# A planned attention and MLP kernel: three score groups of the last batch in one 64-row stretch, a plan that counts descriptors, and another order of the first loads

## The chip, the cores and the metric

The kernel runs on one core of one Trainium2 chip. The metric is the device time of one execution in microseconds (us), median of the runs of a kernel. A profile is one further execution recorded by the hardware profiler; its times are counted from the first instruction of its span. Engines: PE is TensorE (PEld its weight loads, SPq and ACTq are the DMA issues of the SyncE and ScalarE queues), ACT is ScalarE, DVE VectorE, POOL GpSimd, SP SyncE.

## What is computed

Sliding-window attention over 8 batches of 8 heads, 576 positions and head size 64, then a two-layer network with squared ReLU over all 4608 tokens:

```python
scores = q @ k.transpose / sqrt(64)              # batch, head, 576 x 576
mask = abs(pos[:, None] - pos[None, :]) <= 32    # else -1e9
attn = softmax(where(mask, scores, -1e9))
x = (attn @ v).transpose(0, 2, 1, 3).reshape(4608, 512)
g = maximum(x @ w_in, 0) ** 2                    # w_in 512 x 2048
out = g @ w_out                                  # w_out 2048 x 512, float32 out
```

Inputs are float32 in DRAM; the matmuls run in bf16 with float32 sums.

## The kernel before

**Tiles.** A batch has three attention groups of 192 queries; group G runs from 0 to 23. A group works on two windows (A and B) of 128 keys. `scores` (line 548) makes both windows' scores for 8 heads: 16 matmuls with 64 rows of contraction (the head size) and 128 columns. Heads with even and odd number lie in rows 0 to 63 and 64 to 127 and write two different PSUM banks; the code calls the two row halves in turn. Both windows fill the whole 128x2048 PSUM tile `at`. ScalarE takes the exponential of 1024 columns for each window (line 573) into one of two tiles `e`, VectorE multiplies with the band mask (line 578) into one of three tiles `pt`, and `pv` (line 606) multiplies with V: 8 matmuls of 65 columns, the 65th of which is the sum of the softmax. They write into the same tile `at`. VectorE divides (lines 625 and 628) into `xa` (64 tokens) and `xb` (128 tokens), and clears half of the tile (line 634).

**From attention to network.** `xturn` transposes `xa` and `xb` into `xt`, features by tokens: for groups 0 to 2 on TensorE, from group 3 on by two DMA transposes on SP's queue (lines 701 and 704). `mm1` (line 721) is the first product for a chunk of tokens: 192 tokens up to token 767, 256 up to 2047, then 512; for 128 features of the hidden layer it takes four matmuls, and 64 for the chunk. ScalarE's ReLU (727) and VectorE's square (730) write `gt`, with hidden features in partitions. `mm2` (741) is the second product for a block u of 128 tokens, in four quarters of four matmuls, each with 128 rows and 512 columns, into PSUM tile `outp` u modulo 2; ScalarE evicts (751) and stores. The last block is cut in three (`mm2_last`, 766).

**Loads.** POOL issues the loads that cast to bf16. The first six groups' Q and K come in pairs of rows (`load_pair`, 410) and are transposed on TensorE (469); batch 0 group 0 comes over SP without a cast. From batch 2 on they come as 128-row pieces (378) and are transposed by DMA on SP (509). The first loads, with W1 and W2 in quarters (440, 445) and V (427), stand in `OPENING`.

**The plan.** Every operation is recorded (`rec`) with engine, cost, key (its due time) and data dependences. `schedule` then plays the program through with a model of engines and DMA rings and at each step gives a free engine the ready operation with the smallest key. The order that comes out, engine by engine, is the program; `emit` puts in semaphore waits. The times of the model are in no instruction: the constants at the top shape the order alone. Attention has keys of 3G - LEAD, the first product token/64, the second 2u + LAG. Where TensorE would stand still early on, `idle` matmuls are put in (313).

In the text, T4b is group 4's second transpose on SP, and so on.

Of the kernel before, what the change touches and what calls it, by code (L numbers as in the profile page):

```python
# [22 lines left out]
LEAD = 13.0  # L23
LAG = 9.0
AHEAD = 9.0
TISS = 1340
TMOVE = 15
NVR = 24
VKEY = 10.0
TSLACK = 3500  # L30
# [4 lines left out]
PQ = 100  # L35
# [4 lines left out]
HOLD = {}  # L40
# [5 lines left out]
HWB = 150  # L46
# [3 lines left out]
FIRST = {}  # L50
T512 = 2048
NBIAS = 1
PKEY = 0.2
MKEY = (-9.5, -6.5)
VSET = (-9.8, -6.8)
ESPLIT = 0
IOTA = -1
OPENING = [("k", 1), ("w1", 0), ("v", 0, 0), ("v", 1, 1), ("q", 1), ("v", 0, 1), ("q", 2), ("k", 2), ("v", 1, 0), ("w1", 1),
           ("w1", 2), ("w1", 3), ("q", 5), ("v", 2, 0), ("v", 2, 1), ("w2", 1), ("k", 3), ("v", 3, 0), ("q", 3), ("w2", 0), ("w2",
           2), ("k", 4), ("v", 3, 1), ("q", 4), ("v", 5, 0), ("v", 5, 1), ("w2", 3), ("hq", 0), ("k", 5), ("v", 4, 0), ("v", 4, 1),  # L60
           ("hk", 0)]
# [3 lines left out]
KC = ((0, 224), (224, 192), (416, 160))  # L65


class Op:
    __slots__ = ("eng", "fn", "deps", "order", "inc", "val", "sem", "dma", "dur", "key", "i",
                 "succ", "left", "ready", "start", "end", "lat", "move", "name", "slack")  # L70


class Prog:
# [5 lines left out]
    def __init__(self, nc):  # L79
        self.nc = nc  # L80
        self.ops = []
        self.writer = {}
        self.readers = {}

    def rec(self, eng, fn, reads=(), writes=(), dma=None, dur=100, key=0.0, move=0, name="", after=None, slack=0, war=()):
# [5 lines left out]
        op.slack = slack  # L91
        op.lat = self.LAT[eng]
# [24 lines left out]

    def schedule(self):
        ops = self.ops
        for op in ops:  # L120
            op.succ, op.left, op.ready = [], 0, 0
# [15 lines left out]
        now = spent = 0.0  # L137

        def done(op, end):
            for s in op.succ:  # L140
                s.ready = max(s.ready, end if op in s.deps or op.eng != s.eng else free[op.eng])
                s.left -= 1
                if not s.left:
                    heapq.heappush(wait[s.eng], (s.ready, s.i, s))

        def serve(until):
            nonlocal now, spent
            while now < until:
# [16 lines left out]
                if it[1] <= 0:  # L165
                    rings[q].pop(0)
                    it[3].end = now + LANDQ + it[3].slack
                    done(it[3], it[3].end)
                    return True
            return False  # L170

        while True:
            best = None
            for e in engs:
                if pool[e]:
# [13 lines left out]
            if serve(t):  # L189
                continue  # L190
            while wait[e] and wait[e][0][0] <= t:
                _, i, op = heapq.heappop(wait[e])
                heapq.heappush(pool[e], (op.key, i, op))
            first = pool[e][0]
            soon = min((w[0] for w in wait[e] if t < HOLDT and w[0] <= t + HOLD.get(e, 0) and w[2].key < first[0] - KMIN), default=None)
            if soon is not None and soon - t < first[2].dur:
                free[e] = soon
                continue
            op = heapq.heappop(pool[e])[2]
# [8 lines left out]
        assert len(out) == len(ops)  # L208
        self.length = max(o.end for o in out)
        at = free["PE"] = 1500  # L210
        for op in sorted((o for o in out if o.eng == "PE"), key=lambda o: o.start):
            gap = min(op.start, WARM, self.idle_end.start) - at
            one = 430 if at < 5000 else 230
            for k in range(int((gap - 60) // one)):
                w = Op()
                w.eng, w.fn, w.dma, w.deps, w.i = "PE", self.idle, None, {self.idle_on}, op.i
                w.inc, w.val, w.sem, w.start, w.end, w.dur, w.key = False, None, None, at + one * k, 0, one, -99
# [5 lines left out]
    def emit(self):  # L223
        nc = self.nc
        engs = {"PE": nc.tensor, "ACT": nc.scalar, "DVE": nc.vector, "POOL": nc.gpsimd, "SP": nc.sync}
        for op in self.ops:
            for d in op.deps:
                if d.dma is None and not (d.eng == "PE" and op.eng == "PE"):
                    d.inc = True
        sems = {e: nc.alloc_semaphore(f"s_{e}") for e in engs}  # L230
# [6 lines left out]
        for op in self.ops:  # L237
            e = engs[op.eng]
            need = {}
            for d in op.deps:  # L240
                if d.dma is None and d.eng == "PE" and op.eng == "PE":
                    continue
                need[d.sem] = max(need.get(d.sem, 0), d.val)
# [27 lines left out]
class Gen:  # L271
# [5 lines left out]
    def alloc(self):  # L277
# [14 lines left out]
        self.PT = [sb(f"pt{i}", [128, 8, 128], BF16) for i in range(3)]  # L292
# [224 lines left out]
    def scores(self, G, ws):  # L517
# [3 lines left out]
        key = 3 * G - LEAD + 0.3 * ws[0]  # L521
# [39 lines left out]
        if G < NBIAS:  # L561
            rd += [t for w in ws for t in tags[w]]
        self.moe = self.p.rec("PE", f, reads=rd, writes=[t for w in ws for t in tags[w]], key=key, dur=190 + 235 * len(ws),
                              name=f"S{G}{'AB'[ws[-1]]}")
        for w in ws:
            n = 2 * G + w
            sc = self.AT[:, 1024 * reg[w]:1024 * reg[w] + 1024]
            e_, pt = self.E[n % 2], self.PT[n % 3]
            if G < NBIAS:
                self.p.rec("ACT", lambda e, pt=pt, sc=sc: e.activation(pt[:].rearrange("p h q -> p (h q)"), sc, ACTF.Exp, scale=0.125),  # L570
                           reads=tags[w], writes=[("pt", n % 3)], key=key, dur=act(1024), name=f"X{G}{'AB'[w]}")
# [7 lines left out]
                       reads=[("e", n % 2), ("mask", mi)], writes=[("pt", n % 3)], key=key, dur=dve(1024),  # L579
                       name=f"M{G}{'AB'[w]}")  # L580

    def pv(self, G, w):
        b, g = divmod(G, 3)
        n = 2 * G + w
        key = 3 * G - LEAD + 0.3 * w + 0.1
        reg = 1 if NBIAS <= G < NSPLIT or G < NDUP and w else 0
        c0 = 1024 * reg
        vt, pt, avp = self.V[G % NV], self.PT[n % 3], self.AT
# [3 lines left out]
        def f(e):  # L592
            if w and G < NDUP:
                for h in range(8):
                    x, y = divmod(h, 4)
                    c = c0 + 512 * x + 65 * y
                    e.matmul(avp[:, c:c + 65], self.PT[(n - 1) % 3][:, 4 * (h % 2) + h // 2, :], vt[:, 0, h, 0:65], start=(y == 0),
# [12 lines left out]
        rd = [("v", G % NV, w), ("vset", G % NV), ("pt", n % 3), "zz"]  # L610
# [4 lines left out]
        if G < NDUP and w:  # L615
            rd += [("pt", (n - 1) % 3), ("v", G % NV, 0)]
# [19 lines left out]
    def xturn(self, G):  # L636
        xa, xb = self.XA[G % 3], self.XB[G % 3]
        key = 3 * G - LEAD + 0.5
# [95 lines left out]
    def mm2(self, u, seg, key):  # L734
# [4 lines left out]
        def f(e):  # L739
            for d in range(4 * seg, 4 * seg + 4):  # L740
# [5 lines left out]
                       writes=[f"outp{u % 2}"], key=key, dur=864, name=f"B{u}.{seg}")  # L746
        if u == 1 and seg == 0 and not XTD:
# [35 lines left out]
    def build(self):  # L783
# [35 lines left out]
        todo = []  # L819

# [3 lines left out]
        for G in range(NG):  # L824
            b, g = divmod(G, 3)
            if b > 1:
                key = 3 * G - LEAD - AHEAD
# [4 lines left out]
                if g and G < NVR:  # L832
                    key = 3 * G - LEAD - 0.5 if G >= VCS else key
                    at(key + 0.01, self.copy_v, G, key - VKEY if G >= VCS else key)
            for t in "kq":
                key = 3 * G - LEAD - (0.6 if b < NTURN else 3)
                for c in (g,) if b < NTURN else PIECES[t][g]:
                    at(key, self.turn_pe if b < NTURN else self.turn_dma, t, b, c, key)
            for ws in ((0,), (1,)) if G < NSPLIT else ((0, 1),):
                at(3 * G - LEAD + 0.3 * ws[0], self.scores, G, ws)  # L840
            for w in range(2):
                at(3 * G - LEAD + 0.3 * w + 0.1, self.pv, G, w)
            at(3 * G - LEAD + 0.5, self.xturn, G)
# [15 lines left out]
        if True:  # L859
            dsems, dcount = p.emit()  # L860
            for s in dsems:
                if s[0] == "o":
                    self.nc.sync.wait_ge(dsems[s], dcount[s])
# [35 lines left out]
```

## Time and profile before

| | |
|---|---|
| runs without a profile | median 301.89 us (301.73 to 302.03, 3 runs) |
| the profiled execution, its own time | 302.86 us |
| its span, first to last instruction | 301.50 us |
| granted TensorE clock, mean | 1.000 |
| TensorE busy | 292.0 us |
| first product (L721), second product (L741) busy | 142.3 us, 134.2 us |
| scores (L548), V products (L606) busy | 15.2 us, 20.1 us |
| DMA packets, bytes | 160060, 39.83 MB |

Busy times of matmuls include a modelled end of each; what a matmul really holds up is seen from the distance to the start of the next. A timeline's row is: start, duration, engine, line, operation, tile written, shape, count; in brackets the idle time before it and what ended it. The row of a wait is: who waited for whom, us in total, times, longest. "DMA to landing" is the time from the start of an issue to the arrival of its data, least, median, most of a line's instructions in the window asked for.

### The profile page before, as it was taken

What the parts mean: (1) busy time and instruction counts of PE and PEld (TensorE: products, weight loads), DVE (VectorE), ACT (ScalarE), POOL (GpSimd) and SP (SyncE); (2) the same over time, 40 slices, a digit from 0 to 9 for tenths busy, and PEclk for the clock granted to TensorE, in tenths of its full rate; (3) what the DMA queues carried; (4) which work ended last, traced back from release to release, by engine and by line L of the source; (5) the groups of instructions that cost most, each with busy time, mean ns of one, the idle gap of its engine ahead of it and who ended that gap; (6) DMA issues with size and microseconds to landing.
All of it is one profiled execution on the core that took longest, in us unless ns stands there. A gap on an engine that the chain in (4) does not pass through costs nothing.

```text
span 301.5 us, 6221 instructions
## 1 busy us (share of the span) xinstructions
PE 292.0 (97%) x2394; PEld 171.4 (57%) x2431; DVE 166.6 (55%) x385; ACT 160.7 (53%) x250; POOL 102.6 (34%) x131
## 2 busy tenths in 40 slices
PE   7899999998999999999999999999999999999997
PEld 2578865846677777755444444444444444444445
DVE  6897785726666767664377756675465322222200
ACT  3587834825567646654566665456546344344312
POOL 8993335406542643654065435340000000000000
PEclk9999999999999999999999999999999999999999
DMA  9999999999998999999999999996211201000112
GB/s 168 176 206 184 195 173 174 171 154 187 189 157 144 163 145 171 142 163 187 206 144 134 158 164 123 197 164 134 63 34 44 81 35 37 35 35 36 37 70 104
DMA packets 160060, 39.83 MB, mean 132 GB/s; under 512 B 149408, under 2 KB 155552, under 8 KB 160032
## 3 DMA queue, kind: packets, MB, share of 16 engines
q0 software_dynamic: 105824, 17.93, 85.3%
q1 hardware_dynamic: 48880, 12.14, 28.8%
q10 hardware_dynamic: 5328, 9.37, 8.9%
q8 instruction: 19, 0.31, 0.5%
q14 instruction: 9, 0.07, 0.1%
HBM read 36.70 MB, written 9.44 MB: 153 GB/s over the span
## 4 chain that ended last, share of the span: by engine, by line
PE 90%; DMA 5%; POOL 3%; issue 1%; ACT 1%; POOLq 0%; ACTq 0%
PE ht L721 41%; PE outp L741 40%; DMA w<-in_moe_w_in_dram 5%; PE at L606 4%; PE at L548 3%; POOL v L427 1%; POOL w L440 1%; PE at L469 1%; PE ht L766 1%; PE outp L766 1%; POOL kpair L410 1%; POOL qpair L410 1%; ACT rt L727 0%; ACT oe L751 0%; ACT oe L776 0%
## 5 line engine op out<-in xcount | busy, mean ns | idle before, releaser
L721 PE MATMUL ht<-xt,w 128*128 128x256 bf16 (+2 forms) x886 | 142.3, 302 | 2.9 <-issue 1.3
L741 PE MATMUL outp<-w,gt 128*128 128x512 bf16 x535 | 134.2, 379 | 1.4 <-issue 0.2
L727 ACT ACTIVATE rt<-ht 128x512 bf16<-128x512 f32 (+1 forms) x152 | 86.4, 578 | 91.0 <-PE ht L721 87.0
L721 PEld LDWEIGHTS ht<-xt,w 128*128 128x128 bf16 x896 | 80.9, 98 | 44.8 <-issue 1.6
L730 DVE TENSOR_TENSOR gt<-rt 128x512 bf16<-128x512 bf16 (+1 forms) x152 | 61.4, 408 | 64.5 <-ACT rt L727 63.0
L741 PEld LDWEIGHTS outp<-w,gt 128*128 128x128 bf16 x560 | 52.3, 98 | 55.8 <-ACT oe L751 1.0
L378 POOL DMA_DIRECT2D kraw<-in_k_dram x30 | 25.3, 849 | 95.8 <-PE at L548 66.9
L573 ACT ACTIVATE e<-at 128x1024 bf16<-128x1024 f32 x46 | 44.9, 1023 | 10.9 <-PE at L548 10.8
L578 DVE TENSOR_TENSOR pt<-e,mask 128x1024 bf16<-128x1024 bf16 x46 | 31.5, 691 | 24.5 <-ACT e L573 24.2
L427 POOL DMA_DIRECT2D v<-in_v_dram x48 | 38.6, 824 | 0.0
L751 ACT ACTIVATE oe<-outp 128x512 f32<-128x512 f32 x35 | 21.1, 602 | 24.9 <-PE outp L741 24.9
L378 POOL DMA_DIRECT2D qraw<-in_q_dram x30 | 25.5, 859 | 0.0
L606 PEld LDWEIGHTS at<-v,pt 128*128 128x128 bf16 x384 | 18.0, 98 | 10.0 <-issue 1.4
L606 PE MATMUL at<-v,pt 128*128 128x65 bf16 x384 | 20.1, 194 | 0.5 <-ACT pt L570 0.5
L628 DVE TENSOR_TENSOR xb<-at,rs 128x512 bf16<-128x512 f32 x24 | 16.6, 691 | 1.0
L628 DVE TENSOR_TENSOR xa<-at,rs 64x512 bf16<-64x512 f32 x24 | 16.7, 695 | 0.8
L625 DVE RECIPROCAL rs<-at 64x8 f32<-64x8 f32 (+1 forms) x48 | 10.1, 209 | 10.2 <-PE at L606 8.6
L548 PEld LDWEIGHTS at<-qt,kt 64*128 64x128 bf16 x384 | 10.8, 94 | 8.3 <-issue 6.5
L548 PE MATMUL at<-qt,kt 64*128 64x128 bf16 x384 | 15.2, 217 | 0.1
L634 DVE MEMSET at<- 64x520 f32 x23 | 11.3, 492 | 3.7 <-DVE xa L628 2.9
L434 DVE COPY v<-v 64x512 bf16<-64x512 bf16 x16 | 6.1, 382 | 7.4 <-PE ht L721 6.1
L773 DVE COPY oe<-ht 128x128 f32<-128x128 f32 x1 | 0.3, 292 | 14.6 <-PE ht L766 14.6
(67 smaller groups left out, 82.9 us busy)
## 6 DMA issues: line engine op xcount, KB each, us to landing
out_dram<-oe ACTq DMA_DIRECT2D x35, 256.0 KB, 3.7
kraw<-in_k_dram POOLq DMA_DIRECT2D x24, 128.0 KB, 5.3
qraw<-in_q_dram POOLq DMA_DIRECT2D x24, 128.0 KB, 5.8
w<-in_moe_w_in_dram POOLq DMA_DIRECT2D x4, 512.0 KB, 11.5
v<-in_v_dram POOLq DMA_DIRECT2D x16, 128.0 KB, 7.1
w<-in_moe_w_out_dram POOLq DMA_DIRECT2D x4, 512.0 KB, 18.7
v<-in_v_dram POOLq DMA_DIRECT2D x16, 96.0 KB, 7.0
v<-in_v_dram POOLq DMA_DIRECT2D x16, 64.0 KB, 6.0
```

Source lines behind the costliest of these rows:

```text
L378: self.p.rec("POOL", lambda e: e.dma_start(raw[0:n, x % 2, :].rearrange("p (h d) -> p h d", h=8), s), writes=[("raw", t, x // 2, x % 2)], ...
L427: self.p.rec("POOL", lambda e, j=j, lo=lo, hi=hi, k0=k0: e.dma_start(vt[lo - k0:hi - k0, j, :, 0:64], self.v[b, :, lo:hi, :].rearrange("h ...
L548: mm = e.matmul(sc[:, 512 * par + 128 * j:512 * par + 128 * j + 128], kt[r:r + 64, j, k0:k0 + 128], q, start=G >= NBIAS, stop=True, skip_g ...
L573: self.p.rec("ACT", lambda e, e_=e_, sc=sc: e.activation(e_[:], sc, ACTF.Exp, scale=0.125), reads=tags[w], writes=[("e", n % 2)], key=key, ...
L578: self.p.rec("DVE", lambda e, pt=pt, ee=ee, mb=mb: e.tensor_tensor(pt[:], ee, mb, ALU.mult), reads=[("e", n % 2), ("mask", mi)], writes=[( ...
L606: mm = e.matmul(avp[:, c:c + 65], pt[:, 4 * (h % 2) + h // 2, :], vt[:, w, h, 0:65], start=(w == 0 and y == 0), stop=True, skip_group_chec ...
L628: self.p.rec("DVE", lambda e: e.tensor_tensor(x[r0:128, :].rearrange("p (x y c) -> p x y c", x=2, y=4), av[:, :, :, 0:64], rb, ALU.mult), ...
L721: mm = e.matmul(ht[:, n * x:n * x + n], self.W1[:, ft, 128 * d:128 * d + 128], self.XT[:, ft, r:r + n], start=(ft == 0), stop=(ft == 3))
L727: self.p.rec("ACT", lambda e: e.activation(rt[:, 0:c], ht[:, 0:c], ACTF.Relu), reads=[f"ht{k % 2}"], writes=[("rt", k % 4)], key=key, dur= ...
L730: self.p.rec("DVE", lambda e: e.tensor_tensor(gt[:, d0:d0 + len(ds), r:r + n], rr, rr, ALU.mult), reads=[("rt", k % 4)], writes=[("gt", s, ...
L741: mm = e.matmul(op[:], gt[:, d, r:r + 128], self.W2[:, d, :], start=(d == 0), stop=(d == 15))
L751: self.p.rec("ACT", lambda e: e.activation(oe, op[:], ACTF.Copy), reads=[f"outp{u % 2}"], writes=[("oe", u % 4)], key=key, dur=act(512), n ...
```

## The change

1. **A chain.** `CHAINS = {21: 3}`: the scores of groups 21, 22 and 23 are one sequence on TensorE. If the operands of the next two second-product blocks are ready in the plan, `fill` takes these blocks' eight quarters out and puts two runs `half_block(u, 0)` and `half_block(u, 1)` between the score groups: 32 matmuls each of 64 rows and 512 columns, row halves in turn, the two blocks in turn. In the first run block u takes rows 0 to 63 and block u+1 rows 64 to 127 of the hidden features, in the second the other way round; the second waits for the first by a semaphore (`fence`). A chain starts when its data is known, and other groups may be held back for it. `pt` has 7 tiles instead of 3, and the V products of the chained groups use both halves of `at` in turn.
2. **Chunks.** Tokens 768 to 1279 come in chunks of 192, 192 and 128.
3. **The plan.** It counts the descriptors of POOL's loads in flight and holds POOL's next load over 1024; other costs for DMA turns and transposes (`PQ`, `HWB`, `TMOVE`), `LEAD` 12.5 and `LAG` 9.5, ScalarE may be held up to 150 ns for a more urgent operation, batches 2, 6 and 7 get other due times.
4. **The opening.** W1's first quarter is issued first, ahead of the iota, then V, K, Q in another order.

What the built program shows: TensorE's instruction count is nearly the same, and in the stretch of group 21 to 23 it has 16 score matmuls, 32 of `half_block`, 16, 32, 16. Blocks 22 and 23 are the ones that the runs compute. POOL's first nine loads are W1's first quarter, V (128 rows), K, Q, V (96), V (128), V (64), Q, K; before, K, W1's first quarter, V (96), V (128), Q, V (128), Q, K, V (64). The other three quarters of W1 follow in both. On SP the transpose of a Q piece of batch 2 now stands between the two transposes of group 5, and the first K piece of batch 2 ahead of those of group 4. On TensorE the chunk at token 768 starts right after the second V product of group 5.

```diff
-LEAD = 13.0
-LAG = 9.0
+LEAD = 12.5
+LAG = 9.5
-TMOVE = 15
+TMOVE = 21
-PQ = 100
+PQ = 80
-HOLD = {}
+HOLD = {'ACT': 150}
-HWB = 150
+HWB = 200
-FIRST = {}
+FIRST = {768: 192, 960: 192, 1152: 128}
-IOTA = -1
-OPENING = [("k", 1), ("w1", 0), ("v", 0, 0), ("v", 1, 1), ("q", 1), ("v", 0, 1), ("q", 2), ("k", 2), ("v", 1, 0), ("w1", 1),
...
+IOTA = 0.5
+OPENING = [('w1', 0), ('v', 1, 1), ('k', 1), ('q', 1), ('v', 0, 0), ('v', 0, 1), ('v', 1, 0), ('q', 2), ('k', 2), ('w1', 1),
...
+NPT = 7
+CHAINS = {21: 3}
+CSTEP = 0.25
+CEARLY = 12
+CHOLD = 10
+CLAST = 4
+READY = 2000
+PATIENCE = 20000
+SOONER = {7: (-1.0, -0.5), 6: (-1.0, -1), 2: (0.0, -0.5)}
+EXTRA = {6: -3, 7: -0.5}
+ROOM = 1024
...
+        def fill(op, t):
+            u = min((u for u, b in self.blocks.items() if b[0].end is None), default=None)
...
+            both = self.blocks[u] + self.blocks[u + 1]
+            deps = {d for b in both for d in b.deps | b.order if d not in both}
+            if not known(deps, t):
+                return None
...
+                h.eng, h.fn, h.dma, h.deps, h.order, h.i, h.key = "PE", self.half_block(u, kind), None, set(), set(), op.i, op.key
...
+            ops[1].fence = ops[:1]
+            ops[0].deps = deps
+            for b in both:
+                b.dead = ops[1]
...
+            seq = [ops[0], op.chain[1], ops[1]] + op.chain[2:]
...
+            if e == "POOL" and pool[e][0][2].dma is not None:
+                need = pool[e][0][2].move[0] + 1
+                while freeing and freeing[0][0] <= t:
+                    used -= heapq.heappop(freeing)[1]
+                if used + need > ROOM:
+                    if freeing:
+                        free[e] = freeing[0][0]
+                    else:
+                        held_back = True
+                    continue
+                used += need
...
-        self.PT = [sb(f"pt{i}", [128, 8, 128], BF16) for i in range(3)]
+        self.PT = [sb(f"pt{i}", [128, 8, 128], BF16) for i in range(NPT)]
...
+    def half_block(self, u, kind):
+
+        gt, w2 = self.GT, self.W2
+
+        def f(e):
+            for d in range(16):
+                for x in range(2):
+                    v = u + (x + kind) % 2
+                    r, r0 = 128 * v % RING, 64 * x
+                    mm = e.matmul(self.OUTP[v % 2][:], gt[r0:r0 + 64, d, r:r + 128], w2[r0:r0 + 64, d, :], start=kind == 0 and d == 0,
+                                  stop=kind == 1 and d == 15, skip_group_check=True)
+            return mm
+
+        return f
+
+    def pos(self, G):
+        x = self.chained.get(G, 0)
+        return 3 * (G - x) + CSTEP * x - EXTRA.get(G // 3, 0)
+
+    def chain(self, G0, n):
+        ops = [self.scores(G0 + x, (0, 1)) for x in range(n)]
+        ops[0].chain, ops[0].urge = ops, 3 * G0 - CHOLD - EXTRA.get(G0 // 3, 0)
+        for x in range(n):
+            for w in range(2):
+                self.pv(G0 + x, w)
+            self.xturn(G0 + x)
...
-        reg = 1 if NBIAS <= G < NSPLIT or G < NDUP and w else 0
+        reg = self.chained[G] % 2 if G in self.chained else 1 if NBIAS <= G < NSPLIT or G < NDUP and w else 0
```

More of the change, by code (lines that the diff above doesn't have):

```diff
@@ L142, in done @@
                 s.left -= 1
-                if not s.left:
+                if not s.left and not s.inner:
                     heapq.heappush(wait[s.eng], (s.ready, s.i, s))
         def serve(until):
-            nonlocal now, spent
+            nonlocal now, spent, used, held_back
             while now < until:
@@ L174, in schedule @@
             for e in engs:
-                if pool[e]:
+                if e == "POOL" and held_back:
+                    continue
+                while pool[e] and pool[e][0][2].dead:
+                    heapq.heappop(pool[e])
+                while wait[e] and wait[e][0][2].dead:
+                    heapq.heappop(wait[e])
+                if e == "PE" and run:
+                    if run[0].left:
+                        continue
+                    t = max(free[e], run[0].ready)
+                elif pool[e]:
                     t = free[e]
@@ L207, in schedule @@
                 done(op, op.end)
-        assert len(out) == len(ops)
+        assert len([o for o in out if not o.name.startswith("H")]) + sum(o.dead is not None for o in ops) == len(ops)
         self.length = max(o.end for o in out)
@@ L242, in emit @@
                     continue
+                need[d.sem] = max(need.get(d.sem, 0), d.val)
+            for d in op.fence:
                 need[d.sem] = max(need.get(d.sem, 0), d.val)
```

166 lines of the change are left out of this document (130 added, 36 removed).

## The prediction

> **What bounds the kernel now.** I read the busy shares first, then the chain of waits, then TensorE's timeline at the places that the change touches. The page:
>
> ```profile
> PE 292.0 (97%) x2394; PEld 171.4 (57%) x2431; DVE 166.6 (55%) x385; ACT 160.7 (53%) x250; POOL 102.6 (34%) x131
> PE   7899999998999999999999999999999999999997
> PE 90%; DMA 5%; POOL 3%; issue 1%; ACT 1%; POOLq 0%; ACTq 0%
> ```
>
> TensorE is busy in every slice, and 90% of the chain that ends last is its own work. So the time is a sum over TensorE: when its dense stretch begins, what each group of matmuls takes, and its few holes. The price of a group, from the chain in order of time (start, us, what), four matmul widths:
>
> ```profile
> 51.79 1.32 PE ht L721 x16
> 74.29 1.75 PE ht L721 x16
> ...
> 274.38 0.86 PE outp L741 x4
> ...
> 297.71 1.80 PE ht L766 x32
> ```
>
> Divided by their counts: 0.0825 us for 192 columns (first row), 0.109 for 256, 0.2155 for 512, 0.0563 for 128. The other engines have cover: ScalarE waits longer for TensorE than any engine waits for another.
>
> ```profile
> ACT rt L727 <- PE ht L721: 87.0, 105, 3.2
> ```
>
> **The chain of the last batch.** Today each group of scores stands alone between 128-row matmuls. Timeline around group 21:
>
> ```profile
> 203.38 1.03 PE L741 MATMUL outp<-w,gt 128*128 128x512 bf16 x4
> ...
> 204.34 0.62 PE L548 MATMUL at<-qt,kt 64*128 64x128 bf16 x16
> ...
> 204.89 1.04 PE L721 MATMUL ht<-xt,w 128*128 128x512 bf16 x4
> 205.00 1.94 ACT L573 ACTIVATE e<-at 128x1024 bf16<-128x1024 f32 x2 [0.82 <-PE at L548]
> ```
>
> Four matmuls from 203.38 free the array at 203.38 + 4 x 0.2155 = 204.24; the scores start at 204.34, so entering costs 0.10 us. The next group starts 0.55 us after the scores. Sixteen 64-row matmuls of 128 columns, two at a time, are 8 x 0.0563 = 0.45, so leaving costs 0.10 too. One after the other they would be 16 x 0.0563 = 0.90, more than the 0.55 there is: the two row halves do run together. The order of instructions after the change shows scores 21, a run of 32 64-row matmuls, scores 22, another 32, scores 23, with nothing between, so the chain is really formed. Two entries and two leavings go: 4 x 0.10 = **-0.40 us**.
>
> The two runs replace eight groups of four 512-column matmuls (blocks 22 and 23): 8 x 4 x 0.2155 = 6.90 us. In pairs they are 2 x 16 x 0.2155 = 6.90: no difference, if a 512-column pair overlaps as the 128-column pair does. That is the unknown; its bounds are 0 and twice the price, 13.8 us, and I take 0, since the scores are the same tiling with the same alternation of row halves and output banks. What is added are waits. Scores 22 need both exponentials of group 21: 1.94 us (row above) against 3.45 us of matmuls between; before them ScalarE has only one eviction and one ReLU left over. The second run waits for the first by a semaphore; 0.45 us of scores lie between, but its first weights can't be fetched ahead. At both waits TensorE itself stands, with all that follows queued behind it; I bound their sum by 0 and 0.2 (the price of an entry, 0.10, at each) and take **+0.1 us**. At the end of the chain the softmax of three groups is multiplied with V one after another; VectorE's mask, reciprocal and scaling work then stands in a row, but first- and second-product groups lie between, some 0.9 us each.
>
> **Narrower first product.** Tokens 768 to 1279 go in chunks of 192, 192 and 128 instead of 256 and 256. A chunk is 64 matmuls: 128 x 0.109 = 14.0 us today; 128 x 0.0825 + 64 x 0.0563 = 14.16 then: **+0.16 us**. The four extra ReLUs and squares lie in ScalarE's 87 us of waiting.
>
> **The hole at 69 us.** The only large hole after the opening. TensorE:
>
> ```profile
> 58.60 0.42 PE L606 MATMUL at<-v,pt 128*128 128x65 bf16 x8
> ...
> 61.04 0.42 PE L606 MATMUL at<-v,pt 128*128 128x65 bf16 x8
> 61.30 5.34 PE L741 MATMUL outp<-w,gt 128*128 128x512 bf16 x23
> ...
> 67.12 1.90 PE L741 MATMUL outp<-w,gt 128*128 128x512 bf16 x8
> 70.14 1.03 PE L721 MATMUL ht<-xt,w 128*128 128x256 bf16 x8 [1.12 <-issue]
> ```
>
> Eight matmuls free the array at 67.12 + 8 x 0.2155 = 68.84; the first 256-wide chunk (token 768) starts at 70.14: 1.30 us lost, and "issue" says that no compute engine released it. It needs tokens up to 1023, so the first 64 rows of attention group 5, which SP transposes by DMA (timeline of SP's queue; then issue to landing of line 701's three and of line 704's three between 50 and 80 us):
>
> ```profile
> 52.78 1.23 SPq L704 DMA_TRANSPOSE xt<-xb  x1
> ...
> 58.26 3.77 SPq L509 DMA_TRANSPOSE kt<-kraw  x2
> 62.07 1.27 SPq L701 DMA_TRANSPOSE xt<-xa  x1
> 63.39 1.31 SPq L704 DMA_TRANSPOSE xt<-xb  x1
> 64.74 1.76 SPq L509 DMA_TRANSPOSE qt<-qraw  x1
> ```
> ```profile
> DMA to landing us min/median/max: 6.9/7.4/8.0
> ```
> ```profile
> DMA to landing us min/median/max: 5.5/7.1/7.1
> ```
>
> Issued at 62.07 behind two K transposes, landed 8.0 us later at 70.07: that is the hole. A 192-wide chunk at token 768 needs group 4 only, whose last transpose (52.78) has landed by 59.9, and the new order starts it after group 5's second V product (61.04 here): **-1.30 us**. The next 192 tokens (from 960) need both parts of group 5. In the new order 8 first-product groups of 0.66, five quarter blocks of 0.86, one score group (0.65) and two V products (0.26 each) lie between the second V product of group 5 and that chunk: 10.8 us. The transpose today is issued 63.39 - 61.04 = 2.35 us after the product and lands 5.5 to 7.1 later: 7.9 to 9.5. But the change puts the Q transpose of 1.76 us ahead of it on SP: 9.6 to 11.2, so -1.2 to +0.4 against the work. I take **+0.2 us**.
>
> **The opening.** Its end is set by the first-product weights. POOL's issues, then issue to landing of line 440 (W1's four quarters) and of line 410 (pairs of K and Q), then TensorE:
>
> ```profile
> 0.84 0.23 POOL L316 IOTA dif<- 128x128 f32 x1 [0.39 <-POOLq L884]
> 1.41 0.91 POOL L410 DMA_DIRECT2D kpair<-in_k_dram  x1 [0.34 <-issue]
> 2.31 0.78 POOL L440 DMA_DIRECT2D w<-in_moe_w_in_dram  x1
> ...
> 8.71 2.26 POOL L440 DMA_DIRECT2D w<-in_moe_w_in_dram  x3
> ```
> ```profile
> DMA to landing us min/median/max: 7.4/11.5/13.9
> ```
> ```profile
> DMA to landing us min/median/max: 6.1/16.0/22.9
> ```
> ```profile
> 11.09 0.43 PE L606 MATMUL at<-v,pt 128*128 128x65 bf16 x8 [0.45 <-ACT pt L570]
> ...
> 14.14 0.42 PE L597 MATMUL at<-v,pt 128*128 128x65 bf16 x8
> ...
> 17.27 0.83 PE L721 MATMUL ht<-xt,w 128*128 128x192 bf16 x8
> ...
> 24.25 1.48 PE L721 MATMUL ht<-xt,w 128*128 128x192 bf16 x16 [0.43 <-DMA w<-in_moe_w_in_dram]
> ```
>
> The fourth quarter of W1, the third of the issues from 8.71 (0.75 apart), goes out at 10.2 and lands 13.9 us later at 24.1, and the group that needs it starts at 24.25. The new order has the same nine loads ahead of the last three quarters, only permuted, so the queue holds the same bytes before it. But POOL now issues a weight load before the iota: the queue can start where the iota stood, 1.41 - 0.84 = 0.57 us earlier at most. Bounds: 0 and -0.57; I take **-0.3 us**. What is late instead: K of group 1 (first today) goes behind W1's first quarter and a V tile, the first V tile from third to fifth, so the V product at 11.09 slips by about 1 us; the second one, at 14.14, need not: its V tile keeps its place, and it now follows the first one directly. Between the first product at 17.27 and the group at 24.25 stand six groups of 0.66, two V products of 0.26, two half score groups (4 x 0.056 + 0.20 = 0.43 each) and eight transposes (0.45): 5.8 us of work in 7.0. So a first product that comes up to 1.2 us late is still hidden by the wait for W1. The iota comes about 0.8 us later, so do the masks and the bias; the K transposes that follow wait for K itself:
>
> ```profile
> 6.80 0.63 ACT L398 ACTIVATE kraw<-oe 112x512 bf16<-112x512 f32 x1 [1.55 <-DMA oe<-in_k_dram]
> ```
>
> K lands at 6.8, after the bias products even then; without that cover the iota's 0.8 would go on the path. The limit on descriptors is in the plan alone; it adds no instruction and costs nothing but through the orders above.
>
> **The sum.** -0.40 + 0.1 + 0.16 - 1.30 + 0.2 - 0.3 = **-1.54 us**. The profiled execution has a span of 301.50 and a time of 302.86, so 1.36 us lie around the span; the sum makes it 299.96 and 301.32. The runs without a profile have a median of 301.89, 0.97 below the profiled time; I take the same difference of 1.54 from it: **300.4 us**.
>
> **The rivals.**
>
> *The weights of a 64-row run are not hidden.* If a row half cannot load new weights while its own matmul runs, each of the 32 pair slots grows by a load, at most 0.094 us:
>
> ```profile
> L548 PEld LDWEIGHTS at<-qt,kt 64*128 64x128 bf16 x384 | 10.8, 94 | 8.3 <-issue 6.5 <-ACT qt L497 0.4 <-DVE v L363 0.4
> ```
>
> 32 x 0.094 = 3.0 us, so 300.35 + 3.0 = 303.4: slower than before. It decides from 0.048 us a slot (1.54 / 32). Against it: by the same price the scores would take 8 x (0.056 + 0.094) = 1.2 us, not 0.55. For it: no row shows a 64-row run at 512 columns. Chance 0.10. The Trainium skill, page "TensorE: Matmul & The Clock Gate", section "The mechanism", says that weight loads overlap matmuls in flight only where the row group differs; by that rule this rival would come true, and the score rows here speak against it.
>
> *The halves do not run together at 512 columns*: 6.9 us more, 307.2. The scores speak against it. 0.02.
>
> *The hole moves.* SP is in an almost unbroken row of transposes from 52.78 to 66.5. If the chunk at 960 or the one after it waits for as long as the one at 768 does today, the 1.30 comes back: 301.89 - 0.40 + 0.1 + 0.16 - 0.3 = 301.5, no change. For it: the margin above is -1.2 to +0.4 with a queue that is full. Against: a smaller chunk asks for less at once. 0.18.
>
> *The opening gets later.* Today K of group 1 lands at 1.41 + 6.1 = 7.5 and W1's first quarter behind it at 2.31 + 7.4 = 9.7, so that quarter holds the queue for about 2.2 us. If all of batch 0 slips by that, 1.2 us of it are hidden, and the other 1.0 and the lost 0.3 make 300.35 + 1.3 = 301.6, no change. For it: K and the V tiles do go behind it. Against: V's second tile, which releases the V product at 14.14, has the same bytes before it. 0.07.
>
> *More than that*: the whole 0.57 in the opening (-0.27 beside the sum) and no wait in the new places (-0.3): 300.35 - 0.57 = 299.8. 0.10.
>
> **How the numbers follow.** The forecast, from that to 301.0 (its own doubtful terms at their bad ends: 0.1, 0.2 and 0.3), has 0.53, the others as given. About 0.2% (0.6 us) is what a measurement of this kernel can tell from no change: below 301.3 is faster, above 302.5 slower. Faster: 0.53 + 0.10 and a third of the hole and opening rivals (partly true), 0.08: 0.71; slower: both 64-row rivals, and 0.01 of the hole's: 0.13; same: the rest, 0.16. The range 299.3 to 302.5 leaves out the 64-row rivals and a thin end below.
>
> **What would show it.** Right: the two runs of 32 take 3.45 us each and the score groups between them show no idle time before; no "issue" hole before the chunk at 768 and less than 0.5 us before 960; the fourth W1 quarter lands a little before 24.1. Wrong: runs of 5 us or more, a matmul cadence over 0.13 us in them; a new wait of 1 us or more on L721 near 73; a dense stretch that begins after 24.3; waits of TensorE for the exponentials inside the chain.

## The result and the profile after

The changed kernel takes 300.93 us (median of 22 runs, 300.54 to 303.03), the kernel before 302.02 us on the same chips (22 runs, 301.5 to 303.3): a ratio of 0.9967, 95% interval 0.9956 to 0.9978. It is faster by 1.09 us; forecast were 1.54 and 300.4 us. Its profiled execution took 300.68 us with a span of 299.3, 2.18 below the first profile of before: twice the difference of the medians.

The page of the changed kernel, busy shares:

```profile
PE 292.0 (98%) x2493; PEld 173.8 (58%) x2528; DVE 166.8 (56%) x389; ACT 161.5 (54%) x254; POOL 102.3 (34%) x131
```

TensorE still sets the end, with the same busy time and 90% of the chain that ended last. It has some 100 matmuls more than before (2493 records against 2394): 64 from the narrower chunks, 32 from the two runs. The gain is in what lies between its groups. First the chain, TensorE's timeline (start, length, what; L680 are the scores, L726 the runs of 64 rows):

```profile
213.70 1.03 PE L883 MATMUL ht<-xt,w 128*128 128x512 bf16 x4
214.66 0.62 PE L680 MATMUL at<-qt,kt 64*128 64x128 bf16 x16
215.12 3.62 PE L726 MATMUL outp<-w,gt 64*128 64x512 bf16 x32
218.57 0.61 PE L680 MATMUL at<-qt,kt 64*128 64x128 bf16 x16
219.02 3.62 PE L726 MATMUL outp<-w,gt 64*128 64x512 bf16 x32
222.47 0.61 PE L680 MATMUL at<-qt,kt 64*128 64x128 bf16 x16
223.24 1.67 PE L883 MATMUL ht<-xt,w 128*128 128x512 bf16 x7 [0.16 <-issue]
```

Each run holds TensorE for 3.45 us (215.12 to 218.57), 0.108 us a matmul, so two overlap all along. The scores between take 0.45, the bare work; 0.10 us is left at the entry (213.70 + 4 x 0.2155 = 214.56, start 214.66). No wait stands inside. The last row has 7 matmuls of a group of 8: one record is missing ahead of it, and its 0.16 is no wait. ScalarE's exponentials of group 21 start at 215.46 and end at 217.40, 1.2 us before scores 22 need them:

```profile
215.46 1.94 ACT L707 ACTIVATE e<-at 128x1024 bf16<-128x1024 f32 x2
```

Now the place of the old hole, and the chunks behind it (L903 is the second product, L768 the V product, L883 the first product):

```profile
62.26 0.42 PE L768 MATMUL at<-v,pt 128*128 128x65 bf16 x8
62.52 1.48 PE L883 MATMUL ht<-xt,w 128*128 128x192 bf16 x16
...
71.50 0.82 PE L883 MATMUL ht<-xt,w 128*128 128x192 bf16 x8
...
73.02 0.82 PE L883 MATMUL ht<-xt,w 128*128 128x192 bf16 x8
...
87.66 1.95 PE L883 MATMUL ht<-xt,w 128*128 128x128 bf16 x32
```

The chunk at 768 starts straight behind the V product at 62.26. Its last eight matmuls are those at 71.50, and the chunk at 960 starts at 73.02, with no idle time before it. Group 5's second transpose, issued at 65.39 as planned behind the Q transpose, lands in 4.3 us, at 69.7, not in the 5.5 to 7.1 of the prediction:

```profile
65.39 1.26 SPq L866 DMA_TRANSPOSE xt<-xb  x1
```
```profile
DMA to landing us min/median/max: 4.3/4.3/4.3
```

The chunk of 128 columns takes its 1.8 us for 32 matmuls, the 0.056 each that the sum used. Last the opening, POOL's first issues and the group that needs the fourth W1 quarter:

```profile
1.26 0.91 POOL L572 DMA_DIRECT2D w<-in_moe_w_in_dram  x1 [0.81 <-POOLq L1053]
...
8.67 2.30 POOL L572 DMA_DIRECT2D w<-in_moe_w_in_dram  x3
```
```profile
DMA to landing us min/median/max: 7.1/11.1/13.6
```
```profile
23.90 1.48 PE L883 MATMUL ht<-xt,w 128*128 128x192 bf16 x16 [0.26 <-DMA w<-in_moe_w_in_dram]
```

The queue starts 0.15 us earlier than before (1.26 against 1.41), and the last three quarters go out at 8.67 instead of 8.71. The group starts 0.35 us earlier here; whether the order does that, one profile can't say.

### The profile page after: what moved, and what is told of

It is laid out like the page before. It is cut to its first block, busy times and chain, and to the rows that moved or that the text cites. A ratio compares the mean times of both kernels' runs of the same rounds, so it can differ in the third digit from the quotient of the medians.

```text
span 299.3 us, 6420 instructions
## 1 busy us (share of the span) xinstructions
PE 292.0 (98%) x2493; PEld 173.8 (58%) x2528; DVE 166.8 (56%) x389; ACT 161.5 (54%) x254; POOL 102.3 (34%) x131
## 4 chain that ended last, share of the span: by engine, by line
PE 90%; DMA 5%; POOL 3%; issue 1%; ACT 0%; POOLq 0%
PE ht L883 41%; PE outp L903 38%; DMA w<-in_moe_w_in_dram 5%; PE at L768 4%; PE at L680 4%; PE outp L726 2%; POOL v L559 1%; POOL w L572 1%; PE at L601 1%; PE ht L929 1%; PE outp L929 1%; POOL qpair L542 1%; POOL kpair L542 0%; ACT oe L914 0%; ACT oe L939 0%
## 5 line engine op out<-in xcount | busy, mean ns | idle before, releaser
L883 PE MATMUL ht<-xt,w 128*128 128x192 bf16 (+3 forms) x952 | 139.0, 293 | 1.0 <-issue 0.3
L903 PE MATMUL outp<-w,gt 128*128 128x512 bf16 x503 | 124.4, 379 | 1.6 <-issue 0.5
L883 PEld LDWEIGHTS ht<-xt,w 128*128 128x128 bf16 x960 | 83.2, 98 | 42.4 <-ACT rt L889 0.4
L903 PEld LDWEIGHTS outp<-w,gt 128*128 128x128 bf16 x528 | 49.1, 98 | 51.4 <-ACT oe L914 0.3
L768 PEld LDWEIGHTS at<-v,pt 128*128 128x128 bf16 x384 | 18.1, 98 | 8.7 <-DVE at L796 0.5
L768 PE MATMUL at<-v,pt 128*128 128x65 bf16 x384 | 20.1, 194 | 0.0
L680 PE MATMUL at<-qt,kt 64*128 64x128 bf16 x384 | 15.3, 217 | 0.3 <-DVE mask L469 0.3
L680 PEld LDWEIGHTS at<-qt,kt 64*128 64x128 bf16 x384 | 11.1, 94 | 7.7 <-issue 6.5
L445 PE MATMUL outp<-zz 128*128 128x512 bf16 x24 | 7.8, 453 | 1.4 <-DVE zz L439 1.2
```

The lines of the kernel that those rows point to most:

```text
L680: mm = e.matmul(sc[:, 512 * par + 128 * j:512 * par + 128 * j + 128], kt[r:r + 64, j, k0:k0 + 128], q, start=G >= NBIAS, stop=True, skip_g ...
L768: mm = e.matmul(avp[:, c:c + 65], pt[:, 4 * (h % 2) + h // 2, :], vt[:, w, h, 0:65], start=(w == 0 and y == 0), stop=True, skip_group_chec ...
L883: mm = e.matmul(ht[:, n * x:n * x + n], self.W1[:, ft, 128 * d:128 * d + 128], self.XT[:, ft, r:r + n], start=(ft == 0), stop=(ft == 3))
L903: mm = e.matmul(op[:], gt[:, d, r:r + 128], self.W2[:, d, :], start=(d == 0), stop=(d == 15))
```

## The experiments

A ratio is to the kernel before, run beside it, with its 95% interval. Line numbers are the kernel's own: the kernels made from before have L721 for the first product, L741 for the second, L606 for V.

**How long is the hole? Before, twice more; after, once more.** No edit.

> The kernel before, profiled once more. Its first profile took 302.86 us, 0.84 above the median of its runs, and lost 2.18 us to the profile of the changed kernel where the medians differ by only 1.09. Theory P: the first profile was a long one, and in a typical execution the hole before the chunk at token 768 is smaller: the span is about 300.7 us, with a hole of 0.6 us or less there. Rival Q: the hole is 1.2 to 1.3 us in every execution, span about 301.5, and the changed kernel loses something in its other runs.

> The kernel before, profiled a third time. Its first two profiles lost 1.29 and 0.95 us before the chunk at token 768, at 302.86 and 302.33 us, against a median of 302.1. If the length of this hole is what varies between executions, an execution near the median loses 0.7 to 0.9 us there, and its time less that hole agrees with the other two (301.57 and 301.38) to 0.2 us. Rival: the hole is constant near 1 us and the time varies elsewhere, in the first 28 us above all.

> The changed kernel, profiled a second time. Its first profile took 300.68 us, 0.25 below the median of its runs. If what varies is the loads of the opening, as the profiles of its variants suggest (1.0 to 1.6 us more than the work by the second V product of group 2), the time differs from 300.68 by just the difference there, and no wait appears between 60 and 75 us. Rival: a hole near 70 us appears in some executions of the changed kernel too.

TensorE before the chunk at 768, second profile of before (first two rows) and third (last two):

```profile
67.04 1.90 PE L741 MATMUL outp<-w,gt 128*128 128x512 bf16 x8
69.72 1.03 PE L721 MATMUL ht<-xt,w 128*128 128x256 bf16 x8 [0.78 <-issue]
```
```profile
66.99 1.90 PE L741 MATMUL outp<-w,gt 128*128 128x512 bf16 x8
69.41 1.05 PE L721 MATMUL ht<-xt,w 128*128 128x256 bf16 x8 [0.52 <-DMA xt<-xa]
```

Start of the first row plus 8 x 0.2155, to the start of the second: the hole. The third profile names its releaser, the transpose of `xa`.

| execution | time | group that needs the fourth W1 quarter | hole | time less hole |
|---|---|---|---|---|
| before, first profile | 302.86 | 24.25 | 1.30 | 301.56 |
| before, second | 302.33 | 24.23 | 0.96 | 301.37 |
| before, third | 302.20 | 24.11 | 0.70 | 301.50 |
| after, first | 300.68 | 23.90 | none | 300.68 |
| after, second | 301.12 | 24.35 | none | 301.12 |

Theory P missed at first (0.96, not 0.6 or less), rival Q too (not 1.2 to 1.3). The third profile agrees with the theory set down for it: the hole varies from execution to execution, and in these three the time goes with it; what remains agrees to 0.2 us. By 301.5 of remainder, a run at the medians of this kernel's four sets of runs (302.02, 302.22, 302.11 and 302.45) would have 0.5 to 0.95 us of hole. That is an estimate: runs without a profile show no holes, and the changed kernel, whose profiles have none here, spreads as widely (300.54 to 303.03), so other parts vary too. The changed kernel varies in the opening: its second profile is 0.45 later at the W1 group and 0.44 longer. The two executions nearest to the medians, 302.20 and 301.12, differ by 1.08, as the medians do.

**Three ways to close the hole, each alone in the kernel before.**

```diff
-FIRST = {}
+FIRST = {768: 192, 960: 192, 1152: 128}
```

> The kernel before with the chunks of 192, 192 and 128 at token 768 as the only change. If they alone take the hole at 69 us away: -1.30 + 0.16 = -1.14 us against the profiled span of before, a ratio of 0.996 (0.998 if a typical hole is only half as long). Rival: the hole goes to the chunk at 960 or at 1152, and the 0.16 us for narrower matmuls is all that is left: a ratio of 1.0005 or more, and a wait of about 1 us before a chunk near 73 us.

```diff
-IOTA = -1
-OPENING = [("k", 1), ("w1", 0), ("v", 0, 0), ("v", 1, 1), ("q", 1), ("v", 0, 1), ("q", 2), ("k", 2), ("v", 1, 0), ("w1", 1),
...
+IOTA = 0.5
+OPENING = [('w1', 0), ('v', 1, 1), ('k', 1), ('q', 1), ('v', 0, 0), ('v', 0, 1), ('v', 1, 0), ('q', 2), ('k', 2), ('w1', 1),
...
```

> The kernel before with the changed kernel's order of first loads and its place of the iota as the only change. The traces of the two kernels show the group that needs the fourth W1 quarter at 24.25 and 23.90 us: if the order of loads does that, -0.35 us, a ratio of 0.999. Rival: the gain there comes from other changed costs of the plan, and the order alone moves that group by less than 0.1 us or makes it later: a ratio of 1.000 or more.

```diff
-        ..., reads=[("raw", t, x // 2, x % 2)],
+        ..., reads=[("raw", t, x // 2, x % 2)] + ([("xa", 2)] if b == 2 and c in (2, 3) else []),
```

> The kernel before with only SP's order changed: the two K transposes of batch 2 that stand ahead of group 5's first transpose are told to come behind it (by one more dependence), the chunks stay 256 wide. If the hole at 69 us is the landing of group 5's transpose, issued 3.8 us late behind those two, it goes: about -1.2 us, a ratio of 0.996 (0.998 if a typical hole is half as long), at no cost for narrower matmuls. Rival: the hole has another cause, for example the landing itself being slowed down by loads in flight: the time stays within 0.1% and the chunk still starts about 1 us late.

Narrow chunks: 301.80 us, ratio 0.9991 (0.9974 to 1.0009). New opening: 301.94 us, 1.0008 (0.9986 to 1.0030). Transpose ahead: 302.23 us, 0.9994 (0.9982 to 1.0007). None is a proven gain, and the transpose ahead, expected at 0.996 to 0.998, falls short of both. The traces say more; TensorE at that place, in this order:

```profile
60.98 1.48 PE L721 MATMUL ht<-xt,w 128*128 128x192 bf16 x16
```
```profile
68.38 1.04 PE L741 MATMUL outp<-w,gt 128*128 128x512 bf16 x4
69.25 1.04 PE L721 MATMUL ht<-xt,w 128*128 128x256 bf16 x8
```
```profile
67.03 1.04 PE L741 MATMUL outp<-w,gt 128*128 128x512 bf16 x4
67.90 1.91 PE L721 MATMUL ht<-xt,w 128*128 128x256 bf16 x16
...
152.68 1.89 PE L721 MATMUL ht<-xt,w 128*128 128x512 bf16 x7
154.85 0.43 PE L606 MATMUL at<-v,pt 128*128 128x65 bf16 x8 [0.28 <-DVE at L634]
```

Each closes the hole (in the first the chunk at 768 starts at 60.98, straight behind a V product). The third shows that SP's order can undo it: issued at 59.93 instead of 62.1, the transpose is in time for a 256-wide chunk. But its plan differs later on, and a V product at 154.85 now waits for a cleared `at`: the eight matmuls ahead of it start at 152.68 and free the array at 154.40, so 0.45 us of the hole are given back there. The second was a surprise: 256-wide chunks, and no wait. Issue to landing of `xa`'s transpose near 62 us, in that kernel, and in the first two profiles of before:

```profile
DMA to landing us min/median/max: 5.1/5.1/5.1
```
```profile
DMA to landing us min/median/max: 8.0/8.0/8.0
```
```profile
DMA to landing us min/median/max: 7.4/7.4/7.4
```

With the new order of loads the same transpose lands in 5.1 us instead of 7.4 and 8.0, though it is issued later, at 63.04. The other profiles divide the same way: 6.4 to 8.0 us in the six with the old order of loads, 4.0 to 5.2 in the seven with the new one. In the plan the order of loads also changes the order of SP's transposes. SP's queue, before (first row) and after:

```profile
51.25 1.25 SPq L509 DMA_TRANSPOSE kt<-kraw  x1
```
```profile
47.31 1.19 SPq L641 DMA_TRANSPOSE kt<-kraw  x1
51.17 1.39 SPq L863 DMA_TRANSPOSE xt<-xa  x1
```

The `kt` rows are the first K piece of batch 2. With the old order it goes out between the two transposes of group 4, at 50.9 to 51.9 in all six profiles; with the new one ahead of both, at 47.3 to 48.2 in all seven. In the first profiles of both kernels SP's transposes land in the order of their issue, and the last K piece ahead of group 5's lands at 68.5 before (issued at 60.0, 8.5 us) and at 66.9 after (61.2, 5.7 us). So the queue ahead of group 5's transpose is through 1.6 us sooner, though the transpose itself is issued 0.7 us later (62.73 against 62.07). No run moves that piece alone, so this is a likely cause and not a shown one.

**The same parts taken out of the changed kernel.** Chunks of 256 again (`FIRST = {}`); the old `OPENING` and `IOTA`; no chain (`CHAINS = {}`).

> The changed kernel with chunks of 256 tokens at 768 and 1024 again. Its order has 24 second-product matmuls, a score group and 4 more of them between group 5's second V product and the chunk at 768, as before the change, but all starts about 1.2 us later against SP's transposes. Theory A, the prediction's: the narrow chunks take the hole away, so it comes back: 0.96 (as in the second profile of before) to 1.30 less the 0.16 of the narrow matmuls, +0.8 to +1.1 us, a ratio of 0.9995 or more to before. Theory B, from the run of before with the new order of loads, where the wide chunk at 69.25 did not wait: the other order of the first 62 us takes the hole away, and the narrow chunks only cost: -0.16 us against the changed kernel, a ratio of about 0.996.

> The changed kernel with the old order of first loads and the old place of the iota. Theory A: the order of loads gives the 0.35 us at the fourth W1 quarter and no more: the group that needs it starts at about 24.25 again, ratio to before 0.998. Theory B: the order of loads also moves group 5 against SP's transposes, and without it waits appear between 60 and 75 us, so more than 0.6 us is lost, ratio 0.999 or more. Rival to both: the order of loads is worth nothing, ratio 0.9967.

> The changed kernel with CHAINS empty: groups 21 to 23 have their scores alone between 128-row matmuls, blocks 22 and 23 are eight groups of four 128-row matmuls; all ahead of group 21 stays in its order. By the prediction two entries to and two exits from 64-row tiling come back, +0.40 us, ratio to before 0.998, and the order of the profile before group 21 keeps its times. Rival: the chain gives nothing in its kernel because what follows it was late for something else: the last V product ends at the same time as with the chain, ratio 0.9967.

Wide chunks: 300.98 us, 0.9961 (0.9947 to 0.9976): theory A falls. TensorE, and the landing of the transpose:

```profile
68.50 1.04 PE L903 MATMUL outp<-w,gt 128*128 128x512 bf16 x4
69.38 1.04 PE L883 MATMUL ht<-xt,w 128*128 128x256 bf16 x8
70.48 0.43 PE L768 MATMUL at<-v,pt 128*128 128x65 bf16 x8
```
```profile
DMA to landing us min/median/max: 4.0/4.0/4.0
```

No hole before 69.38. The 0.16 us that B expected as a gain did not come either: eight 256-wide matmuls from 69.38 end at 70.25, the V product starts at 70.48, and those 0.23 us undo it.

Old opening: 301.53 us, 0.9978 (0.9967 to 0.9989). By the ratios that is 0.3 us above the changed kernel, with intervals that overlap; the kernel with wide chunks, run beside it, took 0.55 less. The profile shows the loss neither where theory A put it (the W1 group starts at 24.09, not 24.25) nor where theory B did (no wait between 60 and 75 us). A new wait stands at W2:

```profile
44.19 1.90 PE L903 MATMUL outp<-w,gt 128*128 128x512 bf16 x8 [0.47 <-DMA w<-in_moe_w_out_dram]
```

No chain: 301.30 us, 0.9969 (0.9957 to 0.9982). The runs alone decide nothing here: the ratio is next to the rival's 0.9967, and its interval holds the prediction's 0.998 too. The profiles say more. Up to the first V product of group 20 the order is the same, and from there to the last group, after (first two rows) and without the chain:

```profile
207.15 0.42 PE L768 MATMUL at<-v,pt 128*128 128x65 bf16 x8
...
295.37 1.95 PE L929 MATMUL ht<-w,gt 128*128 128x128 bf16 x32
```
```profile
207.67 0.42 PE L768 MATMUL at<-v,pt 128*128 128x65 bf16 x8
...
296.31 1.95 PE L929 MATMUL ht<-w,gt 128*128 128x128 bf16 x32
```

That is 88.22 us with the chain and 88.64 without: 0.42. The second profile of the changed kernel and the one with wide chunks, which have the chain too, show 88.21 and 88.21. The 0.52 us by which the first row is later come from the opening.

**Row halves one after the other.** The same 32 matmuls, half by half:

```diff
-            for d in range(16):
-                for x in range(2):
+            for x in range(2):
+                for d in range(16):
```

> The changed kernel with the loops of half_block exchanged: 16 matmuls on one row half, then 16 on the other, instead of in turn. The work is the same. If two 64-row matmuls run together only because they are issued in turn on the two row halves, each run of 32 takes 32 x 0.2155 = 6.9 us instead of 3.45, and the span is 6.9 us longer, about 306.2. If the rule is that a row half's weights can be fetched only while the other half computes, it is longer still: a load of up to 0.094 us for each of 64 matmuls, 6 us more. Rival: the order doesn't matter, since the matmuls queue up by row half: 3.45 us and no change.

One execution, the profiled one: 305.83 us, span 304.5. TensorE's timeline, then matmuls of the run in windows of 2 us (count in brackets):

```profile
215.27 5.58 PE L726 MATMUL outp<-w,gt 64*128 64x512 bf16 x29
220.48 0.23 PE L680 MATMUL at<-qt,kt 64*128 64x128 bf16 x1
...
228.40 1.67 PE L883 MATMUL ht<-xt,w 128*128 128x512 bf16 x7 [0.16 <-issue]
```
```profile
215.30:217.30 2.00, 2.00 (x10) 0.90 (x11) 1.00 0.35 131
217.30:219.30 2.00, 2.00 (x15) 0.91 (x14) 1.00 0.00 0
```

From the first run's start to the first product behind the chain are 13.13 us instead of 8.12: +5.01, not +6.9. Inside a half 10 matmuls fit in 2 us, 0.2 us each, so they go one by one; in the window where the halves meet there are 15, since some of the second half start under the end of the first. Turn by turn is what makes the run free; in series it costs 5. The exchange also takes away the turns of the two output banks, so this run doesn't tell row halves from banks.

**Two tries at a faster kernel.** A second chain (`CHAINS = {18: 3, 21: 3}`), and W1's last quarters ahead of group 2's K:

```diff
-..., ('q', 2), ('k', 2), ('w1', 1), ('w1', 2), ('w1', 3), ('q', 5),
+..., ('q', 2), ('w1', 1), ('w1', 2), ('w1', 3), ('k', 2), ('q', 5),
```

> The changed kernel with a second chain, groups 18 to 20, ahead of the one of 21 to 23. If each chain saves 0.40 us and nothing else, 0.4 us less than the changed kernel, a ratio to before of 0.9955. Rival: a chain needs other TensorE work behind it for the softmax to catch up; after the second chain the order has its V products one behind the other with little between, so TensorE waits for VectorE there, 2 to 3 us are lost and the ratio is 1.002 to 1.007. Both chains' runs of 32 should take 3.45 us either way.

> The changed kernel with the load of group 2's K put behind the last three quarters of W1 instead of ahead of them. The wait that is left in the opening (0.26 us for the fourth quarter in the profile, 0.3 to 0.5 in others) should go: up to -0.4 us, a ratio of 0.9955 to 0.9965. Rival: the plan then takes group 2's scores later, and attention, not W1, limits the stretch from 25 to 45 us: new waits for V products or second-product weights, ratio above 0.998.

Two chains: 313.38 us, 1.0369 (1.0350 to 1.0388), worse than the rival expected. Behind its second chain:

```profile
242.27 0.61 PE L680 MATMUL at<-qt,kt 64*128 64x128 bf16 x16
...
251.82 0.62 PE L768 MATMUL at<-v,pt 128*128 128x65 bf16 x8 [2.59 <-DVE at L796]
252.67 7.25 PE L883 MATMUL ht<-xt,w 128*128 128x512 bf16 x23 [0.22 <-issue]
```

From 242.27 to 252.67 are 10.4 us for 0.55 of scores and six V products of 0.26: some 8 lost. The first V product waits for the exponential, and those behind it for VectorE's work on the one before, with nothing between.

W1 first: 305.44 us, 1.0119 (1.0087 to 1.0151). The plan then reorders the whole stretch to 60 us, and TensorE waits longer, and for more:

```profile
22.95 0.82 PE L883 MATMUL ht<-xt,w 128*128 128x192 bf16 x8 [0.85 <-DMA w<-in_moe_w_in_dram]
...
36.85 1.04 PE L903 MATMUL outp<-w,gt 128*128 128x512 bf16 x4 [0.72 <-DMA w<-in_moe_w_out_dram]
```

No variant beats the changed kernel; with wide chunks it is as fast.

## Why the prediction was right, and where it was not

The direction was right, and the sum 0.45 us too large (1.54 against 1.09), above all by the term for the hole. That the rest came out so near is in part luck: 0.3 us of new waits and 0.3 us from the opening were both expected, neither came, and they cancel.

*The chain, -0.40.* Right: from the last 128-row matmul's end (214.56) to the first product behind (223.24, less one missing record of 0.2155) the chain takes 8.46 us, against 3 x 0.65 + 6.90 = 8.85: -0.39. Without it 0.42 us come back in the profile; the runs are too coarse to show it.

*Halves run together, weights hidden.* Right; the rival's 3.0 us did not come. The run of halves in series speaks against it once more: 10 matmuls of one row half in 2 us leave no room for 0.094 of weights each. The Trainium skill, page "TensorE: Matmul & The Clock Gate", section "The mechanism", says in one place that weight loads overlap matmuls only where the row group differs, and in another that they can also go to a background weight buffer; these windows disagree with the first and agree with the second.

*Waits in the chain, +0.1, and at 960, +0.2.* Neither came. The exponentials are done 1.2 us early, and the second transpose of group 5, at 69.7, lands 3.3 us before the chunk at 960 starts at 73.02.

*Narrower first product, +0.16.* Right in price, but the chunks bought nothing in this kernel: with wide ones it takes 300.98 us. The 0.16 saved there is lost again by a V product that starts 0.23 us late.

*The hole, -1.30.* The term that was off. The mechanism was right: SP's transpose of group 5 behind two K transposes (the transpose ahead closes it; the third profile names it). The size came from one execution, 0.84 us above the median of its kernel, and the hole is part of why it was: 1.30, 0.96 and 0.70 in three profiles, by the estimate above 0.5 to 0.95 at the medians. The prediction saw that its profile stood 0.97 above the runs and carried the whole difference over unchanged. The cure was wrong too: the narrow chunks would close it, but the new order of loads does so without them. Why the transpose then lands 2 to 4 us sooner is not settled; the place of the first K piece on SP is the best lead. Nor does any run measure what the hole alone is worth: the three kernels made from before that close it gain 0 to 0.4 us in the medians, none clear of noise.

*The opening, -0.3.* Not there. In the seven profiles with the new order (before with the new opening, the changed kernel twice, and with wide chunks, without chain, with halves in series and with two chains) the W1 group starts at 23.87, 23.90, 24.35, 24.07, 24.52, 23.97 and 24.13, mean 24.12; in the six with the old one (before three times, with narrow chunks and with the transpose ahead, and the changed kernel) at 24.25, 24.23, 24.11, 23.99, 24.16 and 24.09, mean 24.14. The step failed at its start: with no iota ahead of it POOL's first load still goes out no sooner than 1.26, 0.15 us earlier and not up to 0.57, and of that only 0.04 is left when the last three quarters go out. What the profiles show of its worth lies later: in the changed kernel with the old order W2 is late at 44 us, and in the kernel before the new order has `xa`'s transpose in time.

With measured sizes, for the pair of executions near the medians: -0.39 + 0.16 - 0.70, and +0.17 in the opening (second V product of group 2 at 28.49 and 28.66), make -0.76 of the -1.08. The other 0.3 stays open; the waits left in these profiles are of 0.2 us and less, and I can assign it to none of them.

The descriptor limit changes no order: the program planned without it is the same on every engine.

## What to carry to other kernels

Before a hole is put into a sum at full length, see how the profiled execution stands to the median of its runs: a wait for DMA varies from one execution to the next, and a long execution shows long holes. A hole can be closed from either side, by needing the data later or by landing it sooner; take out one cure at a time, or the wrong part gets the credit. A change in the order of loads can change the order of another queue, and the queue is the place to look when a landing moves. A chain of score groups saves only its entries and exits, and needs enough other matmuls behind it for the softmax to catch up.

## What the runs showed of the hardware

With two chains TensorE works little from 242 to 252 us, and the clock falls. Windows of 2 us (PE busy, PEld, DVE, ACT, POOL, then the granted clock):

```profile
244.00:246.00 2.00, 0.84 (x16) 0.63 (x16) 1.80 (x5) 1.39 (x2) 0.00 (x0) 1.00 0.33 123
246.00:248.00 2.00, 0.58 (x11) 0.42 (x12) 1.83 (x5) 0.00 (x0) 0.00 (x0) 0.68 0.52 164
248.00:250.00 2.00, 1.13 (x16) 0.81 (x15) 1.82 (x5) 0.00 (x0) 0.00 (x0) 0.50 0.28 54
...
256.00:258.00 2.00, 2.00 (x8) 0.71 (x6) 0.43 (x2) 1.09 (x2) 0.00 (x0) 0.76 0.00 0
```

It falls to half between 246 and 248 (a mean of 0.68 puts it at 246.7), some 4 us after sparse work begins at 242.7, and stays there, four microseconds into dense work, until about 257. The 23 matmuls recorded from 252.67 to 259.75 take 7.08 us instead of 23 x 0.2155 = 4.96: 2.1 us that the stall costs after its end. The Trainium skill, page "TensorE: Matmul & The Clock Gate", section "Part 1: The HAM clock gate", says that the clock drops to half after an idle window of about 3.4 us and needs as long of work to return; the trace agrees to within a microsecond, and shows that a window need not be idle: 0.84 us of busy time in the 2 us from 244 on did not hold the clock up.

The overlap of row halves reaches over the end of a group: in series, five or six matmuls of the next half, or the next scores (220.48, while the run still goes on), start under the last ones of the other half.
